# A decode block fed by one load stream: K and V in tiles of 32 KB per partition, wm and wq as one transfer each, c over eight partitions

## The chip, the cores and the metric

One core of one Trainium2 chip. The metric is the device time of one execution in microseconds, the median of several executions. In the profiles PE is the matrix engine, PEld its weight loads, DVE the vector engine, ACT the scalar engine, POOL GpSimd, and SP the engine that issues the loads. HBM is the memory that the loads read, SBUF the on-chip memory of 128 partitions that they fill. Each load is spread over 16 DMA engines; a *packet* is one piece that one of them moves, here one row of one partition. The records of the load queue before hold 10,114 rows and 1,202 writes of 4 bytes: 16 for each of the 75 large transfers and one for each of the two small ones, so each engine makes one per large transfer. They are called *completion writes* here, and the trace has as many *completion increments* of a large transfer, 16. Faster or slower is given from 2% on, with a 95% interval.

## The reference, cut to what matters

One token attends to a cache of 32,768 keys in 8 groups of 4 query heads, with an adaptive layer norm before it and a small ReLU layer behind it:

```python
x = A_x                                                  # [1, 1, 512]
mod = (silu(c) @ w_mod).reshape(1, 6, 1, -1)             # sa, ca, ga, sb, cb, gb
h = layernorm(x) * (1 + ca) + sa
q = h @ wq                                               # 32 heads of 128
p = softmax(q @ k.T * 128 ** -0.5)                       # k, v: [8, 32768, 128] bf16, 4 query heads share one
x = x + ga * ((p @ v) @ wo)
h = layernorm(x) * (1 + cb) + sb
x = x + gb * (relu(h @ w1) @ w2)
```

K and V are 8 x 8.39 MB each, 134 MB together. With w_mod, wq, wo, w1 and w2 149.4 MB go into the core for 512 numbers that come out. Nothing is used twice.

## The kernel before

All loads go through one ring of eight slots of 16 KB per partition, in a fixed order, on one queue. A load is issued when the last reader of the tile that lay in its slot is done.

```python
TK = 64                                                  # positions of a partition per step; NTILE = 4 steps a head
kv = A_k_cache[0].rearrange("g (p u j) d -> g u p j d", p=P, j=TK)
ring = ctx.enter_context(tc.tile_pool(name="ring", bufs=8))
...
stream = [("wm", 0), ("wm", 1), ("wq", 0), ("wq", 1)]
stream += [("k", 0, u) for u in range(NTILE)]
for g in range(LAST):
    for u in range(NTILE):
        stream += [("k", g + 1, u), ("v", g, u)]
stream += [("v", LAST, u) for u in range(NTILE - 1)]
stream += [("wo", 0), ("wo", 1), ("v", LAST, NTILE - 1), ("wo", 2)]
stream += [("w1",)] + [("w2", i) for i in range(len(W2P))]
...
def scores(g, u):                                        # K tile: DVE transposes a half, PE multiplies by q
    for half in range(2):
        nc.vector.transpose(out=KTt[:].bitcast(F32), in_=Ksb[:, 32 * half:32 * half + 32, :]...)
        # 8 matmuls [128 x 128] x [128 x 512] into S_ps
...
def pv(g, u):                                            # V tile: 16 matmuls of 512 columns, 16 probabilities each
...
for g in range(Hkv):
    for u in range(NTILE):
        scores(g + 1, u)                                 # if there is a next head
        if g == LAST and u == NTILE - 1: project(0); project(1)
        pv(g, u)
    softmax(g + 1); normalise(g)
project(2)                                               # then layer norm, w1, w2, store
```

Of the kernel before, what the change touches and what calls it, by code (L numbers as in the profile page):

```python
# [9 lines left out]
BF16 = mybir.dt.bfloat16  # L10
F32 = mybir.dt.float32
ACT = mybir.ActivationFunctionType
ALU = mybir.AluOpType
# [4 lines left out]
def kernel(  # L18
# [14 lines left out]
    nc = tc.nc  # L33
    P = 128
    _, _, D = A_x.shape
    _, Hkv, Sk, Dh = A_k_cache.shape
    Hq = A_wq.shape[1] // Dh
# [17 lines left out]



    kv = A_k_cache[0].rearrange("g (p u j) d -> g u p j d", p=P, j=TK)
    vv = A_v_cache[0].rearrange("g (p u j) d -> g u p j d", p=P, j=TK)
    wm_v = w_mod.rearrange("(p kt) n -> p kt n", p=P)  # L60
    wq_v = A_wq.rearrange("(p kt) n -> p kt n", p=P)
    def wo_v(i):
# [6 lines left out]

    front = ctx.enter_context(tc.tile_pool(name="front", bufs=1))  # L70
    mask4 = front.tile([P, 32], F32, name="mask4_sb")[:, 0:REP]
    ring = ctx.enter_context(tc.tile_pool(name="ring", bufs=8))
    const = ctx.enter_context(tc.tile_pool(name="const", bufs=1))
    ktpool = ctx.enter_context(tc.tile_pool(name="ktpool", bufs=3))
    spool = ctx.enter_context(tc.tile_pool(name="spool", bufs=2))
# [5 lines left out]
    def small_ps(shape, name):  # L81
        return ps_small.tile(shape, F32, tag="small", name=name)
# [4 lines left out]
    def load(key):  # L87
        kind = key[0]
        if kind == "wm":
            t = ring.tile([P, KT // 2, 6 * D], BF16, tag="slot", name="wm_sb")  # L90
            src = wm_v[:, 2 * key[1]:2 * key[1] + 2, :]
        elif kind == "wq":
            t = ring.tile([P, KT // 2, Hq * Dh], BF16, tag="slot", name="wq_sb")
            src = wq_v[:, 2 * key[1]:2 * key[1] + 2, :]
        elif kind == "k":
            t = ring.tile([P, TK, Dh], BF16, tag="slot", name="Ksb")
            src = kv[key[1], key[2]]
        elif kind == "v":
            t = ring.tile([P, TK, Dh], BF16, tag="slot", name="Vsb")
            src = vv[key[1], key[2]]  # L100
        elif kind == "wo":
            t = ring.tile([P, WOP[key[1]][1] * REP, D], BF16, tag="slot", name="wo_sb")
            src = wo_v(key[1])
        elif kind == "w1":
            t = ring.tile([P, KT, Dff], BF16, tag="slot", name="w1_sb")
            src = w1_v
        else:
            a0, n = W2P[key[1]]
            t = ring.tile([P, n, FB, D], BF16, tag="slot", name="w2_sb")
            src = w2_v[:, a0:a0 + n]  # L110
        stream_dma(t[:], src)
        loaded[key] = t

    def stream_dma(dst, src):
        i = nc.sync.dma_start(out=dst, in_=src)  # L115
        tc.stamp_issue_order_token(i.ins, "sp_stream")

    stream = [("wm", 0), ("wm", 1), ("wq", 0), ("wq", 1)]
    stream += [("k", 0, u) for u in range(NTILE)]
    for g in range(LAST):  # L120
        for u in range(NTILE):
            stream += [("k", g + 1, u), ("v", g, u)]
    stream += [("v", LAST, u) for u in range(NTILE - 1)]
    stream += [("wo", 0), ("wo", 1), ("v", LAST, NTILE - 1), ("wo", 2)]
    stream += [("w1",)] + [("w2", i) for i in range(len(W2P))]
    pos = [0]

    def need(key):
        while key not in loaded:
            load(stream[pos[0]])  # L130
            pos[0] += 1
        return loaded[key]


    need(("wm", 0))
    xc_row = const.tile([1, 2, D], BF16)
    stream_dma(xc_row[:, 0, :], c)
    stream_dma(xc_row[:, 1, :], A_x[0])
    need(("wm", 1))

    ident_bf = const.tile([P, P], BF16)
    make_identity(nc, ident_bf[:])
# [36 lines left out]
    oT_sb = const.tile([P, Hq], BF16)  # L179
    oA = [const.tile([P, n * REP, P // (n * REP)], BF16, name=f"oA{i}") for i, (_, n) in enumerate(WOP)]  # L180

    xc_ps = small_ps([P, 2, KT], "xc_ps")
    for i in range(2):
        cols = xc_row[:, i, :].rearrange("o (p kt) -> o kt p", kt=KT)
        for kt in range(KT):
            nc.tensor.matmul(  # L186
                xc_ps[:, i, kt:kt + 1], lhsT=cols[:, kt, :], rhs=ident_bf[0:1, 0:1], start=True, stop=True,
            )
    xc = const.tile([P, 2, KT], F32)
    nc.vector.tensor_copy(out=xc[:], in_=xc_ps[:])  # L190
    cT, xT = xc[:, 0, :], xc[:, 1, :]
# [41 lines left out]
    siluT = const.tile([P, KT], BF16)  # L233
    nc.vector.tensor_tensor(out=siluT[:], in0=cT, in1=sig[:], op=ALU.mult)  # L234

    wm_sb = [need(("wm", 0)), need(("wm", 1))]
    modT_ps = small_ps([P, NMOD], "modT_ps")
    for j in range(6):
        for ko in range(KT):
            for kt in range(KT):  # L240
                lhsT = wm_sb[kt // 2][:, kt % 2, j * D:(j + 1) * D].rearrange("p (m ko) -> p ko m", ko=KT)
                nc.tensor.matmul(  # L242
                    modT_ps[:, j * KT + ko:j * KT + ko + 1], lhsT=lhsT[:, ko, :], rhs=siluT[:, kt:kt + 1],
                    start=(kt == 0), stop=(kt == KT - 1),
                )
# [31 lines left out]
    )  # L277
    layernorm_T(xT, stat1, hT[:], modT_sb[:, 0:KT], nca[:], "ln1")

    wq_sb = [need(("wq", 0)), need(("wq", 1))]  # L280
    qT_ps = small_ps([P, Hq], "qT_ps")
    for hq in range(Hq):
        for kt in range(KT):
            nc.tensor.matmul(  # L284
                qT_ps[:, hq:hq + 1], lhsT=wq_sb[kt // 2][:, kt % 2, hq * Dh:(hq + 1) * Dh],
                rhs=hT[:, kt:kt + 1], start=(kt == 0), stop=(kt == KT - 1),
            )
    qT_sb = const.tile([P, Hq], BF16)
# [24 lines left out]
    def scores(g, u):  # L313

        if u == 0:
            S_tiles[g] = spool.tile([P, NG, 512], F32, tag="S_g", name="S_g")
            m_tiles[g] = spool.tile([P, NG], F32, tag="m2", name="m2")
        Ksb = need(("k", g, u))
        G = u // 2
        if u % 2 == 0:  # L320
            S_ps_tiles[g] = ps_s.tile([P, 512], F32, tag="s", name="S_ps")
        S_ps = S_ps_tiles[g]
        for half in range(2):
            t4 = (2 * u + half) % 4
            KTt = ktpool.tile([P, 32 * Dh], BF16, tag="KTt", name="KTt")
            nc.vector.transpose(  # L326
                out=KTt[:].bitcast(F32),
                in_=Ksb[:, 32 * half:32 * half + 32, :].rearrange("p j d -> p (j d)").bitcast(F32),
            )
            KTv = KTt[:].rearrange("p (jj h i par) -> p jj h i par", jj=32, h=2, i=32, par=2)  # L330
            for sl in range(2):
                s = 2 * t4 + sl
                for hp in range(4):
                    h, par = hp // 2, hp % 2
                    nc.tensor.matmul(  # L335
                        S_ps[:], lhsT=qbd[g % 2][:, hp, s, :], rhs=KTv[:, 16 * sl:16 * sl + 16, h, :, par],
                        start=(t4 == 0 and sl == 0 and hp == 0), stop=(t4 == 3 and sl == 1 and hp == 3),
                    )
        if u % 2 == 1:
            with tc.high_priority():  # L340
                nc.vector.tensor_scalar(  # L341
                    out=S_tiles[g][:, G, :], in0=S_ps[:], scalar1=1.0, scalar2=None,
                    op0=ALU.mult, op1=ALU.max, accum_out=m_tiles[g][:, G:G + 1],
                )
# [38 lines left out]
    def pv(g, u):  # L383

        PT_g = PT_tiles[g]
        Vsb = need(("v", g, u))
        G, s0 = u // 2, 4 * (u % 2)
        if g == LAST:

            if u == 0:  # L390
                o_tiles[g] = ps_o.tile([P, REP], F32, tag="oT", name="oT_ps", bufs=1)
            for j in range(TK):
                c0 = (16 * G + j % 16) * 32 + REP * (s0 + j // 16)
                nc.tensor.matmul(  # L394
                    o_tiles[g][:], lhsT=Vsb[:, j, :], rhs=PT_g[:, c0:c0 + REP],
                    start=(u == 0 and j == 0), stop=(u == NTILE - 1 and j == TK - 1),
                )
            return

        if u == 0:  # L400
            o_tiles[g] = ps_o.tile([16, 4 * Dh], F32, tag="o", name="o_ps")
        for j in range(16):
            c0 = (16 * G + j) * 32 + REP * s0
            nc.tensor.matmul(  # L404
                o_tiles[g][:], lhsT=PT_g[:, c0:c0 + 16],
                rhs=Vsb[:].rearrange("p (s j) d -> p s j d", j=16)[:, :, j, :],
                start=(u == 0 and j == 0), stop=(u == NTILE - 1 and j == 15),
            )

# [54 lines left out]
    for g in range(Hkv):  # L464
        if g + 1 < Hkv:
            build_qbd(g + 1)
        for u in range(NTILE):
            if g + 1 < Hkv:
                scores(g + 1, u)
            if g == LAST and u == NTILE - 1:  # L470
                for i in range(len(WOP) - 1):
                    project(i)
            pv(g, u)
        PT_tiles.pop(g)
        if g + 1 < Hkv:
            softmax(g + 1)
        normalise(g)
        if g + 1 == sum(WOP[part_of(g)]):
            spread(part_of(g))
# [16 lines left out]
    x1_rows = rows4(x1T[:], x1_ps, "x1_rows")  # L496

    w1_sb = need(("w1",))
    w1_f = w1_sb[:].rearrange("p kt (a m b) -> p kt a b m", m=P, b=FB)
    hidT_ps = small_ps([P, FT], "hidT_ps")  # L500
    for ft in range(FT):
        for kt in range(KT):
# [55 lines left out]
```

## Time and profile before

| | before |
|---|---|
| time, median of 3 | 358.61 us (358.60 to 358.81) |
| span of the profiled run | 356.8 us |
| read from HBM | 149.42 MB |
| load queue, share of 16 engines' span | 98.3% |
| PE, DVE busy | 78%, 53% |

The lines of the profile are in the prediction below. They are read from the outside in: the row DMA has a 9 in every slice but the first and last, so the first question is not which engine is slow but whether the load stream ever stops. The windows by stage answer it, and the time from issue to landing says how much is queued. How many bytes a packet has and how long it took is in the trace's packet records.

### The profile page before, as it was taken

The numbers are of one execution on the slowest core, as the hardware profiler recorded it, in microseconds if no ns is written. First come the engines' busy times: TensorE is split into PE (matmuls) and PEld (weight loads), VectorE is DVE, ScalarE is ACT, GpSimd is POOL, SyncE is SP. The second block draws the span as 40 slices with busy tenths as digits, with TensorE's granted clock in tenths as the row PEclk, the third lists the DMA queues.
The fourth block names the chain that finished last, engine by engine and source line by source line (L and its number), as shares of the span: only waits on it lengthen the run. The fifth ranks groups of instructions, "written<-read, shape, count | busy, mean of one in ns | idle before, by whom it ended". The sixth has DMA issues, their size and how long they took to land.

```text
span 356.8 us, 4268 instructions
## 1 busy us (share of the span) xinstructions
PE 277.3 (78%) x1859; PEld 128.6 (36%) x1859; DVE 188.0 (53%) x209; ACT 31.6 (9%) x74; POOL 8.3 (2%) x13
## 2 busy tenths in 40 slices
PE   0547876997988969976987969996986889786554
PEld 0542332333333333323432423333332333336553
DVE  8419976553844475565654292647555394442011
ACT  1021012003000120002000110012000200003000
POOL 9000000000000000000000000000000000000000
PEclk9999998999899889999999869998998989997555
DMA  8999999999999999999999999999999999999993
GB/s 307 433 432 426 428 433 430 428 434 430 428 435 426 432 434 428 434 430 430 431 430 432 430 429 437 424 432 435 424 434 431 426 435 430 428 432 434 422 414 138
DMA packets 11342, 149.69 MB, mean 420 GB/s; under 512 B 1210, under 2 KB 1212, under 8 KB 2108
## 3 DMA queue, kind: packets, MB, share of 16 engines
q1 hardware_dynamic: 11316, 149.43, 98.3%
q8 instruction: 14, 0.23, 0.2%
q14 instruction: 4, 0.03, 0.0%
q10 hardware_dynamic: 8, 0.00, 0.0%
HBM read 149.42 MB, written 0.00 MB: 419 GB/s over the span
## 4 chain that ended last, share of the span: by engine, by line
DMA 83%; DVE 7%; PE 5%; issue 4%; ACT 0%; SPq 0%; DVEq 0%
DMA Ksb<-in_A_k_cache_dram 66%; DMA Vsb<-in_A_v_cache_dram 9%; DVE KTt L326 6%; DMA w_sb<-in_B_w_dram 6%; PE S_ps L335 2%; PE o_ps L404 2%; DMA wm_sb<-in_w_mod_dram 2%; PE oT_ps L394 1%; DVE PT_g L373 0%; PE oT_ps L421 0%; DVE S_g L341 0%; ACT X L418 0%; PE ffn_ps L515 0%; SPq L115 0%; DVE o_rows L521 0%
## 5 line engine op out<-in xcount | busy, mean ns | idle before, releaser
L326 DVE STREAM_TRANSPOSE KTt<-Ksb 128x2048 f32<-128x2048 f32 x64 | 144.8, 2293 | 46.0 <-DMA Ksb<-in_A_k_cache_dram 45.9
L335 PE MATMUL S_ps<-KTt,qbd 128*128 128x512 bf16 x512 | 137.4, 417 | 40.1 <-DVE KTt L326 38.9
L404 PE MATMUL o_ps<-Vsb,PT_g 128*16 128x512 bf16 x448 | 103.6, 385 | 3.3 <-DVE PT_g L373 3.3
L335 PEld LDWEIGHTS <-qbd 128*128 128x128 bf16 x512 | 52.0, 104 | 115.4 <-issue 70.5
L404 PEld LDWEIGHTS <-PT_g 128*16 128x16 bf16 x448 | 38.4, 91 | 66.5 <-issue 14.9
L341 DVE TENSOR_SCALAR_CACHE_REDUCE S_g<-S_ps 128x512 f32<-128x512 f32 x16 | 11.0, 688 | 46.3 <-PE S_ps L335 46.3
L306 ACT COPY qbd<-qrep_sb 32x128 bf16<-32x128 bf16 x32 | 9.4, 295 | 174.6 <-PE S_ps L335 173.5
L428 DVE TENSOR_TENSOR oT_sb<-oT_ps,Linv 128x4 bf16<-128x4 f32 x8 | 1.3, 163 | 24.6 <-PE oT_ps L394 17.7
L394 PE MATMUL oT_ps<-PT_g,Vsb 128*128 128x4 bf16 x256 | 7.6, 166 | 8.1 <-DMA Vsb<-in_A_v_cache_dram 4.4
L353 DVE TENSOR_REDUCE Mrow<-mT_ps 1x4 f32<-1x128 f32 x8 | 2.2, 278 | 20.4 <-PE mT_ps L351 20.4
L373 DVE STREAM_TRANSPOSE PT_g<-P_g 128x1024 bf16<-128x1024 bf16 x8 | 9.7, 1212 | 4.7 <-ACT P_g L368 4.7
L418 ACT COPY X<-o_ps 16x512 f32<-16x512 f32 x7 | 4.0, 575 | 84.1 <-PE o_ps L404 84.1
L394 PEld LDWEIGHTS <-Vsb 128*128 128x128 bf16 x256 | 7.5, 105 | 8.3 <-DMA Vsb<-in_A_v_cache_dram 4.5
L421 PE MATMUL oT_ps<-osel,X 16*128 16x4 f32 x56 | 7.4, 250 | 3.2 <-ACT X L418 3.2
L368 ACT ACTIVATE P_g<-S_g,nbias 128x1024 bf16<-128x1024 f32 x8 | 9.2, 1148 | 0.2
L421 PEld LDWEIGHTS oT_ps<-osel,X 16*128 16x128 f32 x56 | 6.7, 186 | 4.6 <-ACT X L418 4.6
L154 DVE COPY sel<-ident_bf 128x128 bf16<-128x128 bf16 x4 | 7.8, 3822 | 0.4 <-POOL ident_bf masks.py:199 0.4
L284 PE MATMUL qT_ps<-hT,wq_sb 128*128 128x1 bf16 x128 | 3.7, 165 | 4.4 <-DVE hT L223 2.7
L242 PE MATMUL modT_ps<-siluT,wm_sb 128*128 128x1 bf16 x96 | 3.3, 172 | 4.1 <-DVE siluT L234 4.1
L453 PE MATMUL attnT_ps<-o_sb,wo_sb 128*128 128x1 bf16 x128 | 4.7, 172 | 2.3 <-DMA wo_sb<-in_A_wo_dram 1.9
L186 PE MATMUL xc_ps<-ident_bf,xc_row 1*128 1x1 bf16 x8 | 0.5, 172 | 7.0 <-DMA xc_row<-in_c_dram 7.0
L378 PEld LDWEIGHTS L_ps<-Lexp,ones_f 128*128 128x128 f32 x16 | 4.8, 310 | 2.4 <-issue 2.0
(90 smaller groups left out, 74.0 us busy)
## 6 DMA issues: line engine op xcount, KB each, us to landing
Ksb<-in_A_k_cache_dram SPq DMA_DIRECT2D x32, 2048.0 KB, 34.3
Vsb<-in_A_v_cache_dram SPq DMA_DIRECT2D x32, 2048.0 KB, 32.1
wq_sb<-in_A_wq_dram SPq DMA_DIRECT2D x2, 2048.0 KB, 13.3
wm_sb<-in_w_mod_dram SPq DMA_DIRECT2D x2, 1536.0 KB, 7.6
wo_sb<-in_A_wo_dram SPq DMA_DIRECT2D x1, 2048.0 KB
wo_sb<-in_A_wo_dram SPq DMA_DIRECT2D x2, 1024.0 KB, 30.6
w_sb<-in_B_w_dram SPq DMA_DIRECT2D x1, 1792.0 KB
w_sb<-in_B_w_dram SPq DMA_DIRECT2D x1, 1024.0 KB
```

The lines of the kernel that those rows point to most:

```text
L154: nc.vector.tensor_copy(out=sel[:, hp, :].rearrange("p (a c) -> p a c", a=4), in_=src)
L306: nc.scalar.copy(out=o, in_=i)
L326: nc.vector.transpose(out=KTt[:].bitcast(F32), in_=Ksb[:, 32 * half:32 * half + 32, :].rearrange("p j d -> p (j d)").bitcast(F32),)
L335: nc.tensor.matmul(S_ps[:], lhsT=qbd[g % 2][:, hp, s, :], rhs=KTv[:, 16 * sl:16 * sl + 16, h, :, par], start=(t4 == 0 and sl == 0 and hp = ...
L341: nc.vector.tensor_scalar(out=S_tiles[g][:, G, :], in0=S_ps[:], scalar1=1.0, scalar2=None, op0=ALU.mult, op1=ALU.max, accum_out=m_tiles[g] ...
L368: nc.scalar.activation(out=P_g[:], in_=S_g[:].rearrange("p g f -> p (g f)"), func=ACT.Exp, bias=nbias[:], scale=scale, accum_out=l_g[:],)
L373: nc.vector.transpose(out=PT_g[:], in_=P_g[:])
L378: nc.tensor.matmul(L_ps[:], lhsT=ones_f[:], rhs=Lexp[:], start=True, stop=True)
L394: nc.tensor.matmul(o_tiles[g][:], lhsT=Vsb[:, j, :], rhs=PT_g[:, c0:c0 + REP], start=(u == 0 and j == 0), stop=(u == NTILE - 1 and j == TK ...
L404: nc.tensor.matmul(o_tiles[g][:], lhsT=PT_g[:, c0:c0 + 16], rhs=Vsb[:].rearrange("p (s j) d -> p s j d", j=16)[:, :, j, :], start=(u == 0 ...
L421: nc.tensor.matmul(oT_ps[:], lhsT=X[:, s * Dh:(s + 1) * Dh], rhs=osel[:, s, :], start=(s == 0), stop=(s == 3),)
L453: nc.tensor.matmul(attnT_ps[:, ko:ko + 1], lhsT=wo_sb[:, r, :].rearrange("p (m ko) -> p ko m", ko=KT)[:, ko, :], rhs=o2_tiles[i][:, r:r + ...
```

## The change

Intent: half as many, twice as long rows for the DMA engines, and half as many transfers. The ring keeps its 128 KB: four slots of 32 KB in place of eight of 16. K and V tiles cover two steps, w_mod and wq come whole. The last V tile stays split, so that the end does not wait for 4 MB. Scores of two steps are now computed before the PV of two steps. c is loaded over eight partitions and multiplied by a small identity to be spread.

```diff
-    kv = A_k_cache[0].rearrange("g (p u j) d -> g u p j d", p=P, j=TK)
+    kv = A_k_cache[0].rearrange("g (p j) d -> g p j d", p=P)
...
-    ring = ctx.enter_context(tc.tile_pool(name="ring", bufs=8))
+    ring = ctx.enter_context(tc.tile_pool(name="ring", bufs=4))
...
-            t = ring.tile([P, TK, Dh], BF16, tag="slot", name="Ksb")
-            src = kv[key[1], key[2]]
+            g, steps = key[1], key[2]
+            t = ring.tile([P, TK * len(steps), Dh], BF16, tag="slot", name="Ksb" if kind == "k" else "Vsb")
+            src = (kv if kind == "k" else vv)[g, :, TK * steps[0]:TK * (steps[-1] + 1), :]
...
+    stream = [("wm",), ("wq",)] + [("k", 0, (2 * G, 2 * G + 1)) for G in range(NG)]
     for g in range(LAST):
-        for u in range(NTILE):
-            stream += [("k", g + 1, u), ("v", g, u)]
+        for G in range(NG):
+            stream += [(kind, gg, (2 * G, 2 * G + 1)) for kind, gg in (("k", g + 1), ("v", g))]
+    stream += [("v", LAST, (0, 1)), ("v", LAST, (2,)), ("wo", 0), ("wo", 1), ("v", LAST, (3,)), ("wo", 2)]
...
+    c_row = const.tile([8, D // 8], BF16)
+    stream_dma(c_row[:], c[0].rearrange("(a n) -> a n", a=8))
+    c_bd = ...                                           # c_row times an 8 x 8 identity, on DVE
...
-        for u in range(NTILE):
-            if g + 1 < Hkv:
-                scores(g + 1, u)
-            ...
-            pv(g, u)
+        for G in range(NG):
+            for u in (2 * G, 2 * G + 1):
+                if g + 1 < Hkv:
+                    scores(g + 1, u)
+            for u in (2 * G, 2 * G + 1):
+                ...
+                pv(g, u)
```

More of the change, by code (lines that the diff above doesn't have):

```diff
@@ L54 @@
     eps = 1e-5
-    kv = A_k_cache[0].rearrange("g (p u j) d -> g u p j d", p=P, j=TK)
-    vv = A_v_cache[0].rearrange("g (p u j) d -> g u p j d", p=P, j=TK)
+    kv = A_k_cache[0].rearrange("g (p j) d -> g p j d", p=P)
+    vv = A_v_cache[0].rearrange("g (p j) d -> g p j d", p=P)
     wm_v = w_mod.rearrange("(p kt) n -> p kt n", p=P)
@@ L89, in load @@
         if kind == "wm":
-            t = ring.tile([P, KT // 2, 6 * D], BF16, tag="slot", name="wm_sb")
-            src = wm_v[:, 2 * key[1]:2 * key[1] + 2, :]
+            t = ring.tile([P, KT, 6 * D], BF16, tag="slot", name="wm_sb")
+            src = wm_v
         elif kind == "wq":
-            t = ring.tile([P, KT // 2, Hq * Dh], BF16, tag="slot", name="wq_sb")
-            src = wq_v[:, 2 * key[1]:2 * key[1] + 2, :]
-        elif kind == "k":
-            t = ring.tile([P, TK, Dh], BF16, tag="slot", name="Ksb")
-            src = kv[key[1], key[2]]
-        elif kind == "v":
-            t = ring.tile([P, TK, Dh], BF16, tag="slot", name="Vsb")
-            src = vv[key[1], key[2]]
+            t = ring.tile([P, KT, Hq * Dh], BF16, tag="slot", name="wq_sb")
+            src = wq_v
+        elif kind in "kv":
+            g, steps = key[1], key[2]
+            t = ring.tile([P, TK * len(steps), Dh], BF16, tag="slot", name="Ksb" if kind == "k" else "Vsb")
+            src = (kv if kind == "k" else vv)[g, :, TK * steps[0]:TK * (steps[-1] + 1), :]
         elif kind == "wo":
@@ L111, in load @@
         stream_dma(t[:], src)
-        loaded[key] = t
+        if kind in "kv":
+            for i, u in enumerate(steps):
+                loaded[(kind, g, u)] = t[:, TK * i:TK * (i + 1), :]
+        else:
+            loaded[key] = t[:]
     def stream_dma(dst, src):
@@ L116, in stream_dma @@
         tc.stamp_issue_order_token(i.ins, "sp_stream")
-    stream = [("wm", 0), ("wm", 1), ("wq", 0), ("wq", 1)]
-    stream += [("k", 0, u) for u in range(NTILE)]
+    stream = [("wm",), ("wq",)] + [("k", 0, (2 * G, 2 * G + 1)) for G in range(NG)]
     for g in range(LAST):
-        for u in range(NTILE):
-            stream += [("k", g + 1, u), ("v", g, u)]
-    stream += [("v", LAST, u) for u in range(NTILE - 1)]
-    stream += [("wo", 0), ("wo", 1), ("v", LAST, NTILE - 1), ("wo", 2)]
+        for G in range(NG):
+            stream += [(kind, gg, (2 * G, 2 * G + 1)) for kind, gg in (("k", g + 1), ("v", g))]
+    stream += [("v", LAST, (0, 1)), ("v", LAST, (2,)), ("wo", 0), ("wo", 1), ("v", LAST, (3,)), ("wo", 2)]
     stream += [("w1",)] + [("w2", i) for i in range(len(W2P))]
@@ L132, in need @@
         return loaded[key]
-    need(("wm", 0))
-    xc_row = const.tile([1, 2, D], BF16)
-    stream_dma(xc_row[:, 0, :], c)
-    stream_dma(xc_row[:, 1, :], A_x[0])
-    need(("wm", 1))
+    wm_sb = need(("wm",))
+    c_row = const.tile([8, D // 8], BF16)
+    stream_dma(c_row[:], c[0].rearrange("(a n) -> a n", a=8))
+    x_row = const.tile([1, D], BF16)
+    stream_dma(x_row[:], A_x[0])
     ident_bf = const.tile([P, P], BF16)
@@ L180 @@
     oA = [const.tile([P, n * REP, P // (n * REP)], BF16, name=f"oA{i}") for i, (_, n) in enumerate(WOP)]
+    one8 = const.tile([8, 1], BF16)
+    nc.gpsimd.memset(one8[:], 1.0)
+    c_bd = const.tile([8, 8, D // 8], BF16)
+    nc.vector.tensor_tensor(
+        out=c_bd[:], in0=c_row[:].unsqueeze(1).to_broadcast([8, 8, D // 8]),
+        in1=ident_bf[0:8, 0:8].unsqueeze(2).to_broadcast([8, 8, D // 8]), op=ALU.mult,
+    )
     xc_ps = small_ps([P, 2, KT], "xc_ps")
-    for i in range(2):
-        cols = xc_row[:, i, :].rearrange("o (p kt) -> o kt p", kt=KT)
+    for i, (rows, one) in enumerate((
+        (c_bd[:].rearrange("a b (m kt) -> a kt (b m)", kt=KT), one8[:]),
+        (x_row[:].rearrange("o (p kt) -> o kt p", kt=KT), one8[0:1, :]),
+    )):
         for kt in range(KT):
-            nc.tensor.matmul(
-                xc_ps[:, i, kt:kt + 1], lhsT=cols[:, kt, :], rhs=ident_bf[0:1, 0:1], start=True, stop=True,
-            )
+            nc.tensor.matmul(xc_ps[:, i, kt:kt + 1], lhsT=rows[:, kt, :], rhs=one, start=True, stop=True)
     xc = const.tile([P, 2, KT], F32)
@@ L234 @@
     nc.vector.tensor_tensor(out=siluT[:], in0=cT, in1=sig[:], op=ALU.mult)
-    wm_sb = [need(("wm", 0)), need(("wm", 1))]
     modT_ps = small_ps([P, NMOD], "modT_ps")
@@ L240 @@
             for kt in range(KT):
-                lhsT = wm_sb[kt // 2][:, kt % 2, j * D:(j + 1) * D].rearrange("p (m ko) -> p ko m", ko=KT)
+                lhsT = wm_sb[:, kt, j * D:(j + 1) * D].rearrange("p (m ko) -> p ko m", ko=KT)
                 nc.tensor.matmul(
@@ L278 @@
     layernorm_T(xT, stat1, hT[:], modT_sb[:, 0:KT], nca[:], "ln1")
-    wq_sb = [need(("wq", 0)), need(("wq", 1))]
+    wq_sb = need(("wq",))
     qT_ps = small_ps([P, Hq], "qT_ps")
@@ L284 @@
             nc.tensor.matmul(
-                qT_ps[:, hq:hq + 1], lhsT=wq_sb[kt // 2][:, kt % 2, hq * Dh:(hq + 1) * Dh],
+                qT_ps[:, hq:hq + 1], lhsT=wq_sb[:, kt, hq * Dh:(hq + 1) * Dh],
                 rhs=hT[:, kt:kt + 1], start=(kt == 0), stop=(kt == KT - 1),
@@ L405, in pv @@
                 o_tiles[g][:], lhsT=PT_g[:, c0:c0 + 16],
-                rhs=Vsb[:].rearrange("p (s j) d -> p s j d", j=16)[:, :, j, :],
+                rhs=Vsb.rearrange("p (s j) d -> p s j d", j=16)[:, :, j, :],
                 start=(u == 0 and j == 0), stop=(u == NTILE - 1 and j == 15),
@@ L466 @@
             build_qbd(g + 1)
-        for u in range(NTILE):
-            if g + 1 < Hkv:
-                scores(g + 1, u)
-            if g == LAST and u == NTILE - 1:
-                for i in range(len(WOP) - 1):
-                    project(i)
-            pv(g, u)
+        for G in range(NG):
[3 more added lines that the diff above has]
+            for u in (2 * G, 2 * G + 1):
+                if g == LAST and u == NTILE - 1:
+                    for i in range(len(WOP) - 1):
+                        project(i)
+                pv(g, u)
         PT_tiles.pop(g)
@@ L498 @@
     w1_sb = need(("w1",))
-    w1_f = w1_sb[:].rearrange("p kt (a m b) -> p kt a b m", m=P, b=FB)
+    w1_f = w1_sb.rearrange("p kt (a m b) -> p kt a b m", m=P, b=FB)
     hidT_ps = small_ps([P, FT], "hidT_ps")
```

## The prediction

> **What bounds the kernel now.** I read the DMA and GB/s rows of the page first, then the queue and chain parts, the table of windows, the issues, and last the trace's records of single DMA packets. From the page of the kernel before:
>
> ```profile
> PE   0547876997988969976987969996986889786554
> DVE  8419976553844475565654292647555394442011
> DMA  8999999999999999999999999999999999999993
> GB/s 307 433 432 426 428 433 430 428 434 430 428 435 426 432 434 428 434 430 430 431 430 432 430 429 437 424 432 435 424 434 431 426 435 430 428 432 434 422 414 138
> ...
> q1 hardware_dynamic: 11316, 149.43, 98.3%
> ...
> DMA 83%; DVE 7%; PE 5%; issue 4%; ACT 0%; SPq 0%; DVEq 0%
> ```
>
> Every slice but the first and the last has DMA at 9 and about 430 GB/s, while PE and DVE stay below. The load queue is busy 98.3% of 16 engines' span; the chain of waits is 83% DMA. The windows by stage say the same (stretch, its length, busy us and instructions of PE, PEld, DVE, ACT, POOL, then the TensorE clock, the DMA share and GB/s):
>
> ```profile
> 120.00:180.00 60.00, 51.59 (x227) 21.86 (x225) 33.60 (x34) 6.34 (x16) 0.00 (x0) 0.94 1.01 431
> 240.00:300.00 60.00, 49.32 (x212) 20.81 (x211) 33.49 (x34) 3.97 (x8) 0.00 (x0) 0.91 1.01 430
> 340.00:353.10 13.10, 8.28 (x243) 7.54 (x243) 2.04 (x14) 0.74 (x3) 0.00 (x0) 0.50 0.85 343
> ```
>
> The DMA share is 1.0 until 340 us and falls only in the last 13 us. So the queue never runs dry: the kernel is one stream of 149.4 MB from 1.76 us (first packet) to 352.98 us, plus a fixed end of 3.8 us. How deep the queue is shows in the issues (KB each, median us from issue to landing) and the chain in order of time (start, us):
>
> ```profile
> Ksb<-in_A_k_cache_dram SPq DMA_DIRECT2D x32, 2048.0 KB, 34.3
> Vsb<-in_A_v_cache_dram SPq DMA_DIRECT2D x32, 2048.0 KB, 32.1
> ```
>
> ```profile
> 296.21 33.26 DMA Vsb<-in_A_v_cache_dram
> 329.47 0.05 issue
> 329.52 1.17 PE oT_ps L394 x38
> 330.69 0.93 issue
> 331.62 0.85 PE oT_ps L394 x26
> 332.47 0.02 issue
> 332.49 20.49 DMA w_sb<-in_B_w_dram
> ```
>
> A 2 MB tile takes 2.097 MB / 430.4 GB/s = 4.87 us alone but lands 34.3 us after its issue: seven tiles queue ahead of it. Even the last 256 KB is issued 20.5 us before it lands. The long DMA pieces of the chain are therefore queueing, not latency; a released buffer is not what the end waits for, the amount of data is.
>
> **The single packets.** In the trace's packet records a load row is one packet. Median durations: 16,384 bytes 611 ns, 14,336: 535, 12,288: 460, 8,192: 309, 2,048: 84, 1,024: 46, and 9 ns for the 4-byte completion write that each engine makes per transfer. A packet starts 4 ns before the end of the one before it, so the period of a 16 KB packet is 607 ns. The line through all of them is 37.65 ns per KiB plus about 8.5 ns, or 4.6 ns when the overlap of 4 ns is taken off. Between 60 and 320 us the mean rate is 430.3 GB/s. Beside the 16 KB packets stand 14 instruction fetches of 16 KB, 0.88 to 0.97 us each; a load packet that meets one takes about 1,100 ns instead of 611. At the end 16 engines are busy until 349.5 us, 9 at 350.25, 5 at 352.25, none at 352.75: the engines have drifted up to 3 us apart, mostly, I think, through these fetches.
>
> [...]
>
> **The change, part by part.**
>
> 1. *Fewer packets.* Before: 64 K/V tiles, 2 wq and the first wo transfer at 128 rows of 16 KB (8,576 packets), 256 of 12 KB, 256 of 8 KB, 128 of 14 KB, 896 of 2 KB, 2 of 1 KB: 10,114. After: 31 K/V tiles (16 K, 15 V) and wq make 4,096 rows of 32 KB, wm 128 rows of 24 KB, two V singles and one wo 384 rows of 16 KB, the rest as before and 8 small ones for c: 5,897. That is 4,217 fewer, 264 per engine, at 4.6 ns: 1.21 us off every engine's stream, if a row of 32 KB is one packet (then about 1,213 ns). The bytes don't change.
> 2. *Fewer completion writes.* 75 large transfers become 42: 33 fewer per engine at 9 - 3.5 = 5.5 ns: 0.18 us. The 33 issues that SP no longer makes (0.33 us each) are off the path, since the queue is 30 us deep.
> 3. *c over eight partitions, wm whole.* c lands behind 3.1 MB instead of 1.6: I expect it at 10.5 us against 7.0. But before, DVE is held by the sel copies and small reductions until 10.5 us, and xc is copied only at 10.56. With one product on DVE (about 0.2 us) and the eight small matmuls (0.5 us) after it, modT starts near 12.5 us instead of 11.6 and gives wm's slot back near 16 instead of 15.3. The queue then holds work until 38 us. Cost at the end: 0.
> 4. *Coarser ring, same 128 KB.* A slot of 4.19 MB takes 9.7 us to come. Its successor in the slot is four tiles on, so its turn comes 3 x 9.7 = 29 us after the first tile landed. A K tile is free after four transposes, 4 x 2.29 = 9.2 us, say 11; a V tile after its 32 products at 0.226 us (16 take 3.62 us), behind the 32 score products of its pair: 14.5 us of PE per pair of 19.4 us, so free about 10 us after landing. Both leave 18 us of slack, where the start of a transfer needs about 1 us (0.74 to 1.76 us at the beginning). Issue to landing should fall from 34 to about 29 us, and nothing stops.
> 5. *Tail.* Worked back from the end at 435 GB/s: last K tile lands at 303, last V pair of head 6 at 313, first V of head 7 at 322.5, its third tile at 327.5, wo at 332 and 334.5, the last V tile at 339.5, wo's last part at 342. The last scores end at 314.5, PV of head 6 at 322, the softmax chain takes 4.8 us (320.05 to 324.87 before), so PV of head 7 starts near 326.6, against 324.9 before, and frees the 4 MB slot at 330.4. There the last V tile is issued, 4 us before its turn at 334.5. w1 is issued near 334.5 for its turn at 342, the last w2 part near 344 for its turn at 350. Tightest slack 4 us; no hole, cost 0. After the last landing the same 3.8 us follow.
>
> Sum: -1.21 - 0.18 + 0 = -1.4 us. 358.6 - 1.4 = 357.2 us.
>
> **Rivals.** (a) *The packets don't grow*: rows of 32 KB are cut into 16 KB, and only the completion writes go: 358.4 us. Against it: every row length from 2 to 16 KB is one packet in this trace; for it: none longer than 16 KB appears. (b) *A wait on a slot takes the place*: ring of four. For it: PE is at 49 to 52 of 60 us, and the last V tile has only 4 us of slack; a stage at a lower granted clock (0.81 from 300 to 340 us) could use that. Each us of hole in the stream is a us at the end; I would give it +1 to +4 us, so 358 to 361. (c) *The drift shrinks or grows*: the time is set by the slowest engine, 3 us behind the fastest; which engines get the instruction fetches may change with the instruction counts[...]. That is worth up to 1.5 us either way: 355.7 to 358.7. (d) *The whole 8.5 ns per packet counts*, not 4.6: -2.2 - 0.3, 356.1 us. The starts 4 ns before the ends speak against it.
>
> **Range and chances.** The centre is 357.2; (c) and (d) widen it down to 355.7, (a) and a small hole of (b) up to 358.9. A gain of over 2% (7.2 us) would need the stream's 149.4 MB in 351.2 - 7.2 = 344 us, 434 GB/s from the first packet to the last with start and drift included[...]; a loss over 2% needs 7 us of holes, which the slack of 18 us in the long stage makes unlikely. Faster 0.02, within 2% 0.96, slower 0.02.
>
> **What would show it.** The load queue should count about 6,580 packets instead of 11,316, the 32 KB packets 1,213 ns; the middle windows should read 432 to 433 GB/s instead of 430 and the DMA share stay 1.0; K's issue to landing should be near 29 us; the chain should still end in queueing for w2. It is wrong if a window's GB/s falls below 425 (a hole, rival b), if packets stay at 16 KB (a), or if the end moves though the middle rate does not (c).

Sum: -1.21 - 0.18 + 0 = -1.39, about -1.4 us, and 358.6 - 1.4 = 357.2 us. The 435 GB/s of part 5 is an estimate from the slope of the packet durations in the trace of before: 16 engines x 1,024 bytes / 37.65 ns = 435.2 GB/s, 1.1% above the 430.3 measured there from 60 to 320 us. The 434 GB/s that a gain of 2% would need is 99.7% of it.

## The result, and the profile after

| | before | after |
|---|---|---|
| time, median of 4 | 358.61 us (358.57 to 358.81) | 357.26 us (356.94 to 357.64) |
| ratio | | 0.9962, 95% interval 0.9944 to 0.9979 |
| packets of the load queue | 11,316 | 6,578 |
| last landing | 352.98 us | 351.9 us |
| mean rate, 60 to 320 us | 430.5 GB/s | 432.3 GB/s |

Ratios here are the mean time of one kernel's runs over that of the other's of the same rounds, so not quite the ratio of the medians quoted. The gain is 0.4%: clear of the noise, and far inside the 2% that counts as the same. A second job with five rounds (e5 below) gave 357.49 us and 0.9968.

The page after, the same rows as before:

```profile
PE   0552875998689885998499849987799859987754
DMA  8999999999999999999999999999999999999993
GB/s 321 442 422 440 431 427 442 429 425 438 435 426 438 431 422 446 427 431 440 424 442 435 422 443 427 431 437 427 431 437 428 427 438 433 424 437 424 408 411 130
...
q1 hardware_dynamic: 6578, 149.43, 97.9%
...
DMA 47%; PE 34%; DVE 14%; issue 3%; ACT 0%; SPq 0%; DVEq 0%
```

The DMA row still has a 9 in every slice but the first and last. Single slices of GB/s jump more than before, because a packet is counted at one time and is now twice as large; the windows are the place to compare. After (stretch, its length, busy us and instructions of PE, PEld, DVE, ACT, POOL, clock, DMA share, GB/s):

```profile
120.00:180.00 60.00, 48.52 (x214) 21.14 (x212) 31.68 (x34) 6.11 (x16) 0.00 (x0) 0.89 1.01 434
240.00:300.00 60.00, 49.48 (x211) 21.14 (x209) 32.77 (x31) 3.75 (x8) 0.00 (x0) 0.86 1.00 432
300.00:340.00 40.00, 31.66 (x395) 18.62 (x393) 12.56 (x18) 3.16 (x5) 0.00 (x0) 0.82 0.99 423
340.00:352.10 12.10, 8.36 (x243) 7.55 (x243) 2.02 (x14) 0.74 (x3) 0.00 (x0) 0.50 0.82 330
```

The middle reads 432 to 434 GB/s in place of 430 and 431. The window from 300 to 340 us reads 423 in place of 429 (423 in e5 and e6 too). That is below the 425 which the prediction named as the sign of a hole, and there is a small one. With each packet counted by the part of it that falls into the window, the rates are 427.4 and 429.8. The packet records place the loss at the last V tile: in the kernel after, eight packets that start between 331.7 and 332.7 us last 700 to 1,491 ns in place of 309 or 611, and from 330 to 334 us the packets exceed the medians of their lengths by 0.23 us per engine, against 0.03 before (0.27 in e5, 0.00 in e1). It fell on the engines that lead. By the completion increments, from the first engine's landing of wo to the first one's of the last V tile it took 5.23 us, from the last to the last 4.84, which is about what eight packets of 607 ns need. So no cost of it can be seen on the engine that ends last. The issues after (KB each, median us from issue to landing):

```profile
Ksb<-in_A_k_cache_dram SPq DMA_DIRECT2D x16, 4096.0 KB, 29.7
Vsb<-in_A_v_cache_dram SPq DMA_DIRECT2D x15, 4096.0 KB, 25.5
```

K lands 29.7 us after its issue, as a queue of three tiles of 9.7 us does; V lands after 25.5, so a V slot comes free about 4 us later than a K slot. The chain of waits in order of time shows where that comes from (start, us, what):

```profile
85.76 0.27 PE mT_ps L359
86.03 7.02 PE o_ps L412 x32
...
123.69 0.27 PE mT_ps L359
...
273.10 30.95 DMA Ksb<-in_A_k_cache_dram
...
330.82 9.35 DMA Vsb<-in_A_v_cache_dram
...
344.27 7.63 DMA w_sb<-in_B_w_dram
```

Up to 157 us this chain runs through PE and DVE without a wait: the first scores start 5 us later than before, as K's first tile is 4 MB, and then compute catches up with the stream. From one head's mT_ps to the next it takes 123.69 - 85.76 = 37.9 us, the stream 38.7 (225.4 - 186.7, two landings of the same K tile of neighbouring heads). So compute gains only 0.8 us per head on the stream. None of this cost time in the long stage, since the queue was never empty there; but it is why the share of PE in the chain went from 5% to 34%. The last V tile was issued at 330.82 us and the last w2 part 7.6 us before its landing, against 20.5 before: the slack in the tail is thinner, and at the last V tile it was gone for the leading engines.

The packet records: 4,096 packets of 32,768 bytes with a median of 1,213 ns, the next starting 3 to 4 ns before the end of the last; 611 ns at 16 KB as before.

### The profile page after: what moved, and what is told of

The parts are those of the page before. It is cut to its first block, busy times and chain, and to the rows that moved or that the text cites. A ratio compares the mean times of both kernels' runs of the same rounds, so it can differ in the third digit from the quotient of the medians. Undisturbed runs are those within 1.5% of the kernel's fastest.

```text
span 355.8 us, 4200 instructions
## 1 busy us (share of the span) xinstructions
PE 274.2 (77%) x1859; PEld 129.9 (37%) x1859; DVE 188.0 (53%) x210; ACT 30.8 (9%) x74; POOL 8.5 (2%) x14
## 3 DMA queue, kind: packets, MB, share of 16 engines
q1 hardware_dynamic: 6578, 149.43, 97.9%
## 4 chain that ended last, share of the span: by engine, by line
DMA 47%; PE 34%; DVE 14%; issue 3%; ACT 0%; SPq 0%; DVEq 0%
DMA Ksb<-in_A_k_cache_dram 42%; PE S_ps L343 18%; PE o_ps L412 12%; DVE KTt L334 11%; DMA Vsb<-in_A_v_cache_dram 3%; DMA w_sb<-in_B_w_dram 2%; PE oT_ps L402 1%; DVE PT_g L381 1%; PE oT_ps L429 1%; DVE S_g L349 1%; PE L_ps L386 0%; SPq L118 0%; PE attnT_ps L461 0%; PE mT_ps L359 0%; ACT X L426 0%
## 5 line engine op out<-in xcount | busy, mean ns | idle before, releaser
L343 PE MATMUL S_ps<-KTt,qbd 128*128 128x512 bf16 x512 | 134.5, 423 | 29.8 <-DVE KTt L334 29.7
L334 DVE STREAM_TRANSPOSE KTt<-Ksb 128x2048 f32<-128x2048 f32 x64 | 142.6, 2279 | 21.1 <-DMA Ksb<-in_A_k_cache_dram 17.0
L412 PE MATMUL o_ps<-Vsb,PT_g 128*16 128x512 bf16 x448 | 99.0, 379 | 0.0
L343 PEld LDWEIGHTS <-qbd 128*128 128x128 bf16 x512 | 53.8, 106 | 104.6 <-issue 53.8
L386 PE MATMUL L_ps<-Lexp,ones_f 128*128 128x4 f32 x16 | 3.9, 314 | 13.0 <-DVE Lexp L384 13.0
L359 PE MATMUL mT_ps<-ident_f,m_p 128*1 128x128 f32 x8 | 2.2, 269 | 8.4 <-DVE m_p L357 8.4
L386 PEld LDWEIGHTS L_ps<-Lexp,ones_f 128*128 128x128 f32 x16 | 3.6, 271 | 13.5 <-issue 13.4
## 6 DMA issues: line engine op xcount, KB each, us to landing
Ksb<-in_A_k_cache_dram SPq DMA_DIRECT2D x16, 4096.0 KB, 29.7
Vsb<-in_A_v_cache_dram SPq DMA_DIRECT2D x15, 4096.0 KB, 25.5
```

Source lines behind the costliest of these rows:

```text
L343: nc.tensor.matmul(S_ps[:], lhsT=qbd[g % 2][:, hp, s, :], rhs=KTv[:, 16 * sl:16 * sl + 16, h, :, par], start=(t4 == 0 and sl == 0 and hp = ...
L386: nc.tensor.matmul(L_ps[:], lhsT=ones_f[:], rhs=Lexp[:], start=True, stop=True)
L412: nc.tensor.matmul(o_tiles[g][:], lhsT=PT_g[:, c0:c0 + 16], rhs=Vsb.rearrange("p (s j) d -> p s j d", j=16)[:, :, j, :], start=(u == 0 and ...
```

## The experiments

Twelve runs were made (e5 is the changed kernel itself), all of them correct against the reference. "Changed" is the kernel after.

### e1: the ring and order of the change, the packets of before

```diff
-        stream_dma(t[:], src)
+        if kind in ("wm", "wq"):
+            for h in range(2):
+                stream_dma(t[:, 2 * h:2 * h + 2, :], src[:, 2 * h:2 * h + 2, :])
+        elif kind in "kv" and len(steps) == 2:
+            for h in range(2):
+                stream_dma(t[:, TK * h:TK * (h + 1), :], src[:, TK * h:TK * (h + 1), :])
+        else:
+            stream_dma(t[:], src)
```

> The changed kernel with its ring of four, its order and its c kept, but every transfer with rows of 32 or 24 KB made as two transfers of half rows: the packets and completion writes of the kernel before. Packet theory (4.6 ns per packet, 5.5 ns per completion write): 10,121 data packets again, time 357.25 + 1.2 + 0.2 = 358.65 us, equal to before within 0.3. Rival, that the ring's order or the coarser slots give the gain: it stays near 357.3. Rival, that the ring of four costs something that the packets hide: above 359.0.

Measured: 358.62 us (358.44 to 359.13), before 358.59, ratio 1.0003 (0.999 to 1.0015). The load queue of e1:

```profile
q1 hardware_dynamic: 11330, 149.43, 98.3%
```

With the packets and transfers of before the whole gain is gone, although ring, slots and order are those of the change. Within the 0.15% of the interval the order and the coarse slots give nothing and cost nothing.

### e2: one transfer per tile, rows of 16 KB

```diff
-            src = (kv if kind == "k" else vv)[g, :, TK * steps[0]:TK * (steps[-1] + 1), :]
+            base = (kv if kind == "k" else vv)[g].rearrange("p (r two c) d -> p r two (c d)", two=2, c=64)
+            nr, r0 = TK * len(steps) // 64, (steps[0] % 2) * (TK // 64)
+            src = base[:, r0:r0 + nr, steps[0] // 2, :]
...                                                      # the tile is viewed to match
```

> The changed kernel with one transfer per 32 KB tile, but each row made of two runs of 16 KB that do not touch in memory (pieces 0 and 2, then 1 and 3, for K and V alike, which only renames the keys): 3,968 packets more, no completion write more. Packet theory: 248 packets per engine at 4.6 ns, +1.14 us, 358.4 us. Rival, that fewer transfers and completion writes give the gain: 357.3 us.

Measured: 358.56 us (358.45 to 358.68), before 358.59, ratio 1.0000 (0.9987 to 1.0012). The load queue of e2:

```profile
q1 hardware_dynamic: 10546, 149.43, 98.2%
```

That is 3,968 packets more than changed, as expected. From the ratios of the two five-round jobs: (1.0000 - 0.9968) x 358.6 = 1.15 us for 248 packets per engine, 4.6 ns each. The two intervals together leave about 0.6 us, so 2.5 ns per packet, and that it meets the predicted 4.6 so closely is partly luck; e9 below is seven times as sensitive. So the packets are enough to carry the gain. Between this run and e1, which adds the completion writes and 16 more packets per engine, there are 0.06 us: the 0.18 us of the completion writes is below what the runs resolve.

### e3, e7, e9: packets of 4 KB, three ways

If a packet costs 4.6 ns, seven more in place of every 32 KB packet must cost 8.2 us. e3 cuts the rows in memory as e2 does, with c=16, so that a transfer reads runs of 4 KB at a pitch of 8 KB.

> As the run before, with runs of 4 KB: 28,544 packets more than the changed kernel, 1,784 per engine. Packet theory: a 4 KB packet lasts 4 x 37.65 + 8.5 = 159 ns with a period of 155 ns; +1,784 x 4.6 ns = +8.2 us, 365.5 us. If the whole 8.5 ns counted: +15.2 us, 372.4. If the cost of a packet is only seen at large ones (drift, fetches): under 360.

Measured: 380.70 us (379.33 to 381.96), ratio 1.0621 (1.0595 to 1.0647), 15 us more than expected. The windows of e3:

```profile
60.00:120.00 60.00, 50.21 (x209) 20.80 (x209) 31.77 (x30) 5.75 (x12) 0.00 (x0) 0.89 1.02 388
120.00:180.00 60.00, 46.28 (x192) 19.20 (x192) 31.75 (x29) 4.24 (x12) 0.00 (x0) 0.89 1.02 396
240.00:300.00 60.00, 50.06 (x221) 20.87 (x219) 32.48 (x31) 3.06 (x8) 0.00 (x0) 0.94 1.02 420
```

The DMA share is 1.02 in the windows shown, but the engines move only 383 (from 20 to 60 us) to 396 GB/s up to 180 us and 420 later, which is what a period of 155 ns gives (16 x 4,096 / 155 = 423). The packet records say the same: median 159 ns as expected, but the mean is 165.6, and 8.4% of the packets from 20 to 60 us and 4.6 to 4.9% from 60 to 180 us last over 160 ns, a few by far (99.9th percentile 884 ns). So the 4 KB packets were not the whole cost; something in this way of reading slows some of them. e7 therefore reads memory in order and makes the cut on the SBUF side:

```diff
-            t = ring.tile([P, TK * len(steps), Dh], BF16, tag="slot", ...)
+            t = ring.tile([P, 4 * len(steps), 16 * Dh + 16], BF16, tag="slot", ...)   # 32 bytes of padding per 4 KB
...
+            stream_dma(t[:, :, 0:16 * Dh], src.rearrange("p (r c) d -> p r (c d)", c=16))
```

(The readers use the padded view; each half tile is transposed in two parts.)

> Packets of 4 KB again, but memory is read in order: the cut is on the SBUF side, by 32 bytes of padding after every 4 KB of a K or V tile (32 more transposes of half size are not: 128 of half size in place of 64, DVE has room). The 4 KB runs of 8 KB pitch gave 380.7 us, with packets of 159 ns median but 165.6 mean. Theory, the order of the memory reads slowed a part of those packets: mean near 159 and 365.5 us (1,784 x 4.6 ns more than changed). Rival, small packets as such are slow in the first 180 us: 380 again.

Measured: 372.45 us (372.12 to 372.69), ratio 1.0387 (1.0373 to 1.0401). Neither number. The slow start is gone, every window from 20 to 300 us reads 412:

```profile
240.00:300.00 60.00, 50.92 (x204) 20.64 (x202) 29.57 (x41) 5.15 (x12) 0.00 (x0) 0.86 1.03 412
```

but its level is too low, and the packets last from 159 to 172 ns, mean 162.7. My padding had made a new difference: seven of eight runs now start in SBUF off a multiple of 256 bytes from the slot's start. That such starts cost time was a guess. e9 pads with 256 bytes (shown against e7):

```diff
-            t = ring.tile([P, 4 * len(steps), 16 * Dh + 16], BF16, tag="slot", ...)
+            t = ring.tile([P, 4 * len(steps) * 2176 - 128], BF16, tag="slot", ...)    # runs at a step of 2176 elements
...                                                      # tv: the view of the 4 KB runs alone
```

> Packets of 4 KB read in order once more, with 256 bytes of padding between the runs instead of 32. The run with 32 bytes gave 372.4 us at a steady 412 GB/s; its packets lasted 159 to 172 ns, mean 162.7, so 3.7 ns more than the line. Theory, the odd starts of the runs in SBUF cost that: now all packets 159 ns, 420 to 422 GB/s, and 357.4 + 1,784 x 4.6 ns = 365.6 us. Rival, 4 KB packets cost more than the line says whatever the start: 372 again.

Measured: 365.99 us (365.70 to 366.17), ratio 1.0203 (1.0189 to 1.0217), against 365.6 expected.

```profile
240.00:300.00 60.00, 50.30 (x211) 20.83 (x211) 32.86 (x47) 5.15 (x12) 0.00 (x0) 0.94 1.02 421
```

Steady 421 GB/s, packets of 159 ns (mean 159.3). Worked out as in e2: (1.0203 - 0.9968) x 358.6 = 8.43 us for 1,784 packets per engine, 4.7 ns each, within 0.4 by the two intervals. The term of the prediction holds over a factor of seven in packets. The step from e7 to e9, 6.5 us, comes from the padding alone, which moved the starts of the runs onto 256-byte steps: the packets took a mean of 159.3 ns in place of 162.7. Why such starts are slower is not shown. That 256 is the step, and not 64 or 128 bytes or the pitch of the runs, was not tested, and 41% of e7's packets (13,488 of 32,768) lasted 159 ns all the same. Why e3's pattern slows packets in the first 180 us and hardly later is open: its reads differ from e9's in memory order and its runs lie without padding in SBUF, and nothing here takes that apart further.

### e4, e5, e6: c in one row

```diff
-    c_row = const.tile([8, D // 8], BF16)
-    stream_dma(c_row[:], c[0].rearrange("(a n) -> a n", a=8))
+    c_row = const.tile([1, D], BF16)
+    stream_dma(c_row[:], c)
-    c_bd = ...
-        (c_bd[:].rearrange("a b (m kt) -> a kt (b m)", kt=KT), one8[:]),
+        (c_row[:].rearrange("o (p kt) -> o kt p", kt=KT), one8[0:1, :]),
```

> The changed kernel with c loaded as one row on one partition again, without the product on DVE. Theory: off the path, queue holds work until 38 us: 357.2 us, within 0.2 of the changed kernel. Rival, that c over eight partitions brings some of the gain: 357.6 or more.

Measured: 357.57 us (357.31 to 357.74), ratio 0.9971, on another chip than the changed kernel's run, so 0.3 us of difference could not be judged. Both once more, on one chip:

> The changed kernel itself, five rounds beside the run without its c form: 357.2 us. With it the difference of the run before (357.57 with c in one row) is judged on one chip.

> c in one row again, on the same chip as the changed kernel. Theory, c is off the path: within 0.2 us of the changed kernel of this job. Rival, c over eight partitions is worth 0.3 us: 0.3 us more again.

Measured: changed 357.49 us (357.32 to 357.60), ratio 0.9968; c in one row 357.38 us (357.21 to 357.46), ratio 0.9965. The c form makes no difference. 357.3 to 357.6 is what to expect from one chip or another.

### e8: three slots

```diff
-    ring = ctx.enter_context(tc.tile_pool(name="ring", bufs=4))
+    ring = ctx.enter_context(tc.tile_pool(name="ring", bufs=3))
```

> The changed kernel with three slots of 32 KB instead of four. Slack theory: a slot's turn comes two tiles, 19.4 us, after the tile in it landed; K is free after 9 us and V after 13, so the long stage still holds (5 us and more) and only the start, where the consumers lag, and the tail, where the last w2 part waits for w1 (1 us of slack), make holes: 358 to 361 us. Issue to landing of K falls to about 20 us. Rival, the ring of four is already at its limit: over 365 us.

Measured: 361.01 us (359.98 to 361.49), ratio 1.0063 (1.0048 to 1.0078), 3.5 us more than changed in the same job. One issue line and two windows of e8:

```profile
Ksb<-in_A_k_cache_dram SPq DMA_DIRECT2D x16, 4096.0 KB, 19.3
```

```profile
60.00:120.00 60.00, 54.26 (x235) 22.80 (x234) 37.15 (x32) 4.73 (x11) 0.00 (x0) 0.91 0.99 425
120.00:180.00 60.00, 47.48 (x202) 20.29 (x201) 32.16 (x34) 6.11 (x16) 0.00 (x0) 0.89 1.00 433
300.00:340.00 40.00, 32.95 (x402) 19.17 (x400) 13.10 (x18) 3.16 (x5) 0.00 (x0) 0.84 0.96 404
```

The long stage holds 433 GB/s with a queue of 19 us; the holes are where they were expected, in the catching-up stage (425) and in the tail (404). So the fourth slot is worth 3.5 us. That the long stage does without it shows that four leave slack there.

### e10 and e11: what pulls the engines apart

The prediction supposed that instruction fetches make the 16 engines drift. The completion increments of a tile's transfer in the trace, one per engine, show the drift: in the kernel before, 1.7 us from the first to the last engine of a tile at 100 us, 2.7 at 285, 3.1 at 330. GpSimd has nothing to do after the start (changed: 8.48 us busy before 20 us, 0.00 in every window after), so idle work was put there:

```diff
+    scr = const.tile([1, 1], F32)
+    for _ in range(2000):            # 1000 in e11
+        nc.gpsimd.memset(scr[:], 0.0)
```

> The changed kernel with 2,000 idle memsets of one element on GpSimd, which has nothing else to do: about 128 KB more instructions to fetch, some eight fetches of 16 KB if they come as the 14 others do, 0.6 us of one DMA engine each. Theory, fetches make the engines drift apart: if all eight meet one engine +5 us, if they spread evenly +0.3 us; the spread of the engines' ends grows with them. Rival, the drift has another source: 357.4 us and the same spread of 2 to 3 us.

Measured: 364.83 us (364.60 to 365.12), ratio 1.0173 (1.0159 to 1.0187), +7.4 us. From the page, the windows and the chain of e10:

```profile
q14 instruction: 20, 0.16, 0.1%
```

```profile
300.00:340.00 40.00, 35.90 (x327) 18.18 (x325) 16.76 (x20) 3.16 (x5) 1.58 (x18) 0.88 0.87 363
```

```profile
337.90 9.78 DMA Vsb<-in_A_v_cache_dram
```

q14 has 20 packets instead of 4: 16 fetches of 8 KB, 131 KB, less than 0.1% of the bytes. That is 65.5 bytes a memset. The 128 KB expected was an estimate; the 14 fetches of 16 KB on q8 before, over PE's 3,742 instructions there, are 61 bytes each. The increments, taken from the trace:

| landing of | changed: at, spread, last behind the one before | e10 |
|---|---|---|
| K tile near 190 us | 186.7 us, 2.35, 0.48 | 191.2 us, 7.01, 4.71 |
| K tile near 270 us | 264.1 us, 2.30, 0.20 | 271.2 us, 9.48, 7.19 |
| last K tile | 304.0 us, 3.54, 0.49 | 311.1 us, 10.72, 7.64 |

So in e10 one engine falls behind the second slowest by 7.6 us, in steps: between 101 and 301.5 us the spread of a tile grows from 3.89 to 10.74 us with 11 fetches, 0.62 us each. A tile's readers start after the last of its 16 increments (in the kernel before the first increment of one K tile came at 34.53 us, the last at 36.40, its transpose started at 36.52). So the last K tile is 7 us late and the last V tile is issued at 337.90 us in place of 330.82. The window from 300 to 340 us drops to a DMA share of 0.87 and 363 GB/s, against 0.99 and 423 in the kernel after. A fetch costs that engine 0.62 us, twice the 309 ns that an 8 KB fetch of q14 lasts in the kernel after; why is open.

> Half of the idle memsets: 1,000. The 2,000 brought 16 more fetches of 8 KB and +7.4 us; in their trace the last K tile landed 7.1 us later than in the changed kernel, 0.44 us per fetch, which is what one engine would lose if it carried all of them. Theory, fetches of one queue sit on one engine and that engine sets the landing of every tile: 8 more fetches, last K tile about 3.5 us later, time 357.4 + 3.5 = 360.9 us. Rival, the memsets themselves[...] or only their last part cost the time: DVE transposes longer than 2.28 us, or no cost at half the number.

Measured: 359.46 us (359.23 to 360.02), ratio 1.0028 (1.0014 to 1.0042), +2.1 us by the ratios, less than the 3.5 expected. The last engine was 3.48 us behind the second last when the memsets ended at about 155 us, then 2.8 at 228 us and 2.3 at 306 us: q14 brought 8 more fetches (12 packets in place of 4) and the distance shrank once the memsets had ended. Why it shrank is not shown. Half the fetches, all early, cost less than half. The last K tile came at 305.8 us, 1.7 later than changed. DVE transposes did not get slower (mean 2,278 ns in e10, 2,277 in e11, 2,279 changed), and the time follows the engine's lag: that the fetches and not the memsets as such are the cost is the reading these numbers support.

### e12: more instructions for PE

```diff
             o_tiles[g] = ps_o.tile([16, 4 * Dh], F32, tag="o", name="o_ps")
+            for _ in range(64):
+                nc.tensor.matmul(o_tiles[g][:, 0:4], lhsT=PT_g[:, 0:16], rhs=Vsb[:, 0, 0:4], start=True, stop=True)
```

> The changed kernel with 64 more small matmuls (four columns, their result overwritten) at the start of each of the first seven heads' PV: 448 matmuls, 896 instructions, 57 KB, 3 or 4 more fetches of 16 KB on the queue that brings PE's instructions. Theory, PE's fetches all sit on one engine too: 0.6 to 0.9 us each, last K tile and time +2 to +3 us, 359.5 to 360.4. Rival, PE's fetches go round over several engines: under +0.8 us, below 358.2. PE itself works about 2 us more per head of 38.8 and stays below the stream.

Measured: 364.78 us (363.95 to 366.58), ratio 1.0177 (1.0155 to 1.0198), outside both expectations. Page and chain of e12:

```profile
q8 instruction: 18, 0.29, 0.3%
...
PE 68%; DVE 15%; DMA 13%; issue 2%; ACT 1%; SPq 0%; DVEq 0%
```

```profile
267.15 1.68 PE o_ps L411 x64
...
337.54 8.87 DMA Vsb<-in_A_v_cache_dram
```

Four more fetches of 16 KB came on q8 (18 in place of 14), 65.5 KB for 896 instructions, so q8 carries PE's; the 57 KB expected was an estimate, near the 59 KB that e10's 65.5 bytes a memset make of as many instructions. But the drift did not grow: the last K tile landed at 303.8 us with a spread of 3.28 us (changed 304.0 and 3.54). No pile-up of PE's fetches on one engine shows. The 7 us come from PE: each block of 64 took 1.68 us, more than the 0.8 us per head that compute has in hand, so PE fell behind the stream from head to head, and the last V tile was issued at 337.54 us. "PE stays below the stream" in the expectation was wrong, and the run shows how near PE is. What it says of the fetches is the drift only, not their cost.

No version faster than both kernels suggested itself: the middle runs at 432 of the 435.2 GB/s that the slope of the packets gives (an estimate: 16 x 1,024 bytes / 37.65 ns), and the changes that remain (longer w2 rows, some 0.15 us by the same term of 4.7 ns x 32 packets) are below the noise. What else stands in the traces is the spread of the engines at the last landing, 2.83 us after; no run tried to reduce it.

## Why the prediction was right, point by point

- **Fewer packets, 1.21 us.** Right. The load queue counts 6,578 packets (about 6,580 predicted), a 32 KB row is one packet of 1,213 ns (predicted to the ns), and e2 and e9 measure 4.6 and 4.7 ns per packet, e9 within 0.4. Rival (d), the whole 8.5 ns, would have made e9 372 us; it was 366.0. Rival (a), cut rows, did not happen.
- **Fewer completion writes, 0.18 us.** Not resolved: e1 and e2 differ by 0.06 us.
- **c and wm.** No cost at the end, shown by e6. On the way two figures were off: the product on DVE took 0.68 us, not 0.2, and modT started at 13.14 us, not 12.5. The queue hid both.
- **Coarser ring.** Right for the long stage, where no hole appears (the one in the tail is below); K's issue to landing was 29.7 us (29 predicted). The slack was too generous: a V tile is free 13 us after it lands and not 10 (four tiles of 9.7 us less 25.5 us from issue to landing), because I added up matmuls and left out the chain between heads (copies, small matmuls, PT's transpose). With them compute takes 37.9 us of each 38.7. It did not matter with four slots in the long stage; it mattered in e12.
- **Tail.** The issues came nearly as predicted: the last V tile at 330.82 us (330.4), w1 at 336.4 (334.5), the last w2 part at 344.3 (344). The slack of 4 us and "no hole" were wrong. The turn of the last V tile was counted at the mean rate, 334.5 us, but the engines are 3 us apart, and the first had wo landed at 332.10 us, 1.3 us after the issue. So the leading engines ran short, and the window from 300 to 340 us fell to 423 GB/s. That the end still came in time is because the engine that ends last had 3.2 us more (wo at 335.33). The last landing moved from 352.98 to 351.9 us, and 3.9 us followed.
- **Drift by fetches (rival c).** It changed the outcome little if at all: the spread at the last landing was 3.18 us before and 2.83 after, and up to 0.35 us of the gain could lie in that. That fetches can go with it is shown by e10 (a lag of 7.6 us with 16 of them); that PE's 14 fetches make the 3 us of the two kernels is only likely, from the spread growing with time and their number not being concentrated (e12). The steps of the spread point to them too: in the kernel before it went from 1.64 to 2.81 us between the tiles that landed at 259.98 and 266.02 us, and a fetch of PE's queue stands at 259.9 us; after, from 2.30 to 3.05 us between 264.08 and 274.58, with a fetch of that queue at 266.7 and one of q14 at 270.8. Most other fetches show no such step.
- **Sum.** -1.4 us predicted, 358.61 - 357.26 = 1.35 measured, and 358.62 - 357.49 = 1.13 in e5's job. The interval of the ratio leaves 0.6 us to either side, so the packet term is what is confirmed; that the sum with the 0.18 us came out to 0.05 us is luck.

## What to carry to other kernels

When the load queue is never empty (98.3% of the 16 engines' span here), take the packet durations for several row lengths: the slope, 37.65 ns per KiB, gives a rate (435.2 GB/s, an estimate) that no window of the loads here exceeded (the highest read 434), the intercept less the overlap, 4.6 ns a packet, is what longer rows could still give, and here that was 1.2 us of 358 for halving the packets. The ring could be made coarser here because in the long stage each slot's turn, 29 us after its tile landed, came later than its last reader, 13 us after for V, plus the start of a transfer, about 1 us; in the tail, counted for the engine that leads and not for the mean, the turn came only 1.3 us after the issue, and packets there lost 0.23 us per engine. Read the margin from issue to landing and from the pace of compute per head, not from busy sums. Where a transfer has to be cut into runs, compare paddings: runs of 4 KB that started on 256-byte steps in SBUF were 6.5 us faster here than runs on 32-byte steps. And do not let an idle engine execute thousands of instructions beside a full load stream without measuring it: 2,000 memsets on GpSimd cost 7.4 us here, 1,000 cost 2.1.
